# Sigmoid attention and a squared-ReLU MLP on one core: keys in tiles of 128 and a rest of 64, the rests of two pairs in quarters of the array

## The chip, the cores and the metric

The kernel runs on one core of a Trainium2 chip. Its time is the device time of one launch in microseconds. The engines are TensorE (PE; its weight loads are PEld), VectorE (DVE), ScalarE (ACT), GpSimd (POOL) and SyncE (SP), which issues all the DMAs of this kernel in one queue, in order.

## The reference

```python
# q, k, v: 8 batches, 12 heads, 448 positions, 64 wide; w_in 768 x 2048, w_out 2048 x 768
scores = np.matmul(q, k.transpose(0, 1, 3, 2)) / np.sqrt(64) - np.log(448)
attn = 1.0 / (1.0 + np.exp(-scores))
x = np.matmul(attn, v).transpose(0, 2, 1, 3).reshape(8 * 448, 768)
r = np.maximum(x @ w_in, 0.0)
out = (r * r) @ w_out
```

The attention weights are sigmoids, so no row is normalised. The two MLP weights arrive as 64-bit floats (two 32-bit words each) and are turned into 32-bit floats on the chip.

## The kernel before

**Attention.** The 12 heads of a batch are handled as 6 pairs, 48 pairs in all; two heads of 64 fill 128 partitions. `load_pair` brings q and k of a pair, transposed, as one tile of 128x896 (448 KB); `split_pair` makes a high and a low part of it in fp32r on VectorE. `scores` multiplies keys by queries: the 448 keys of a pair are cut into four tiles of 112 (`KT, NT = 112, 4`), and for each tile there are three products (high by high, low by high, high by low), each of them for the two heads j, in two halves of the array's rows. So a pair has 4 x 3 x 2 = 24 matmuls of 448 columns in `sc`, a PSUM tile of two banks in 3 buffers. ScalarE takes each tile through the sigmoid into `at`, and `attn_v` sums the four tiles of `at` against v into one PSUM bank `pav` (2 buffers) with 4 x 2 plain fp32 matmuls, the heads in two halves of the array's columns. `put_x` copies `pav` to SBUF on VectorE and stores it to `xd` in DRAM.

`step(n)` sets the order of all that: it loads x of pair n+4 and v of pair n+3, copies and stores the output of pair n-1, splits x of pair n+2, and issues the scores of pair n+1 and `attn_v` of pair n. So TensorE always has one pair's scores ahead of the previous pair's `attn_v`, and within one engine everything stands in the order of the code (`manual_schedule`).

**MLP weights.** Spread over steps 0 to 44, `weights(k)` converts one chunk of words at a time (`load_chunk`, tiles f): two ScalarE instructions (`convert_words`, L125 and L126), then in a later step three on VectorE and one on GpSimd (`convert_join`). Every third k, `sums` makes four sums of the blocks a11, a12, a21, a22 of 128x384 on VectorE and stores the seven blocks that the products need. 49 values of k lie on 45 steps, so that steps 0, 11, 22 and 33 have two of them.

**MLP.** Each of the two products is done for two batches at a time (a group g, four groups) with seven block products in place of eight (1 to 7 in the code), all in fp32r with three matmuls for one product. `gemm1` loads the weights of a block row from `w1`, `gemm2` from `w2`; `load_weights` brings 768 KB or 576 KB and `halve_weights` splits them into a high part (ScalarE, L170) and a low part (VectorE, L171). `x_operands(g)` loads the group's x from `xd` and makes the operands of the seven products by pieces (`make`: a cast and a subtraction for each of the blocks; `sub`: differences t1 to t4). For the first group the pieces stand in and behind the last attention steps, and between the first products (`FIRST_STEPS`, `between`); for the later groups they are made during the second product of the group before.

Tiles come from pools of equal buffers: `op2` (35 of 128x896), `op1` (20 of 128x448), `w` (8 of 128x1536).

Of the kernel before, what the change touches and what calls it, by code (L numbers as in the profile page):

```python
# [22 lines left out]
KT, NT = 112, 4  # L23
# [40 lines left out]
):  # L64

# [73 lines left out]
    def sums(m, i, a, s):  # L139

        if m == 0:
            a11, a12, a21, a22 = (a[:, n] for n in range(4))
        else:
            a11, a21, a12, a22 = (a[:, n] for n in range(4))
        s2, s3, s1, s4 = (s[:, n] for n in range(4))
        nc.vector.tensor_add(out=s1, in0=a21, in1=a22)
        nc.vector.tensor_sub(out=s2, in0=s1, in1=a11)
        nc.vector.tensor_sub(out=s3, in0=a11, in1=a21)
        nc.vector.tensor_sub(out=s4, in0=a12, in1=s2)
        if m == 0:  # L150
            nc.sync.dma_start(out=w1[i][:, 0:2], in_=a[:, 0:2])
            nc.sync.dma_start(out=w1[i][:, 2:6], in_=s)
            nc.sync.dma_start(out=w1[i][:, 6], in_=a[:, 3])
        else:
            d = w2.rearrange("n p i c -> p n i c")[:, :, i]
            nc.sync.dma_start(out=d[:, 0:2], in_=a[:, 0::2][:, 0:2])
            nc.sync.dma_start(out=d[:, 2:6], in_=s)
            nc.sync.dma_start(out=d[:, 6], in_=a[:, 3])

    def load_weights(src, name):  # L160
        n = src.shape[1]
        hi, lo = wide(name + "h", F32R)[:, :n], wide(name + "l", F32R)[:, :n]
        nc.sync.dma_start(out=lo.bitcast(F32), in_=src)
        return hi, lo

# [16 lines left out]
    def load_v(b, p):  # L184
        vt = op2(f"v_{b}_{p}").rearrange("p a s -> p (a s)")[:, : NT * P].rearrange("p (t d) -> p t d", d=P)
        nc.sync.dma_start(out=vt[:KT], in_=v[b, p])  # L186
        return vt
# [7 lines left out]
    def scores(ps, b, p, x):  # L195
        out = []
        for t in range(NT):
            sc = ps.tile([P, 2, 512], F32, tag="sc", bufs=3, name=f"sc_{b}_{p}_{t}")[:, :, :S]
            ks = slice(t * KT, (t + 1) * KT)
            for n, (kp, qp) in enumerate(((0, 0), (1, 0), (0, 1))):  # L200
                for j in range(2):
                    rows = slice(j * D, (j + 1) * D)
                    nc.tensor.matmul(  # L203
                        sc[:KT, j], x[kp][rows, 1, ks], x[qp][rows, 0], start=(n == 0), stop=(n == 2)
                    )
            at = op2(f"at_{b}_{p}_{t}")
            nc.scalar.activation(at[:KT], sc[:KT], AF.Sigmoid, bias=NEG_LOG_S, scale=SCALE)  # L207
            out.append(at)
        return out

    def attn_v(ps, b, p, at, vt):
        pav = ps.tile([P, 512], F32, tag="pav", bufs=2, name=f"pav_{b}_{p}")[:, :S]
        for t in range(NT):
            for j in range(2):
                nc.tensor.matmul(  # L215
                    pav[j * D : (j + 1) * D],
                    vt[:KT, t, j * D : (j + 1) * D],
                    at[t][:KT, j],
                    start=(t == 0),
                    stop=(t == NT - 1),  # L220
                )
        return pav

    def put_x(b, p, pav):
        x = op1(f"xo_{b}_{p}")
        nc.vector.tensor_copy(out=x, in_=pav)  # L226
        return lambda: nc.sync.dma_start(out=xd[b, p], in_=x)

    def split(raw, name, new, vector=False):
        hi, lo = new(name + "h", F32R), new(name + "l", F32R)  # L230
# [4 lines left out]
        nc.vector.tensor_sub(out=lo, in0=raw, in1=hi.bitcast(F32))  # L235
        return hi, lo

    def x_operands(g):
# [5 lines left out]
        def load(n, b, k):  # L244
            r2, r1 = op2(f"x{n}_{g}"), op1(f"y{n}_{g}")
# [3 lines left out]
            raw[n] = (r2, r1)  # L249
# [7 lines left out]
        def make(product, n, vector=False):  # L257
            (h2, l2), (h1, l1) = (split(r, f"{t}{n}_{g}", new, vector) for r, t, new in zip(raw[n], "xy", (op2, op1)))
            ops[product] = [(h2[:, 0], l2[:, 0]), (h2[:, 1], l2[:, 1]), (h1, l1)]

# [25 lines left out]
    x, vt, xs, at, pav, f64, w = {}, {}, {}, {}, {}, {}, {}  # L286
    stores = []
    ops = {}

    def weights(k):  # L290
# [11 lines left out]
        halves = halves[:, :DM], halves[:, DM:]  # L302
# [9 lines left out]
    def step(ps, n):  # L312
# [3 lines left out]
        if n + VA <= last:  # L316
            vt[n + VA] = load_v(*pairs[n + VA])
        if n > 0:
            store = put_x(*pairs[n - 1], pav.pop(n - 1))
            if n <= last - 3:  # L320
                store()
            else:
                stores.append(store)
        if n + SA <= last:
            xs[n + SA] = split_pair(*pairs[n + SA], x[n + SA])
        if n < last:
            at[n + 1] = scores(ps, *pairs[n + 1], xs[n + 1])
# [264 lines left out]
```

## Time and profile before

| | before |
|---|---|
| median of 3 runs (lowest to highest) | 1117.72 us (1116.38 to 1126.99) |
| the profiled execution | 1117.46 us |
| its span | 1115.4 us |
| granted TensorE clock | 1.0 |
| TensorE busy | 1105.8 us, 99% |
| VectorE, ScalarE, GpSimd busy | 70%, 55%, 5% |
| DMA | 202.32 MB, mean 181 GB/s over the span |

In lines of the profile, L12 is line 12 of the kernel; `out<-in` are the program's names with the buffer numbers left out; xN counts the instructions; behind a bar or in square brackets stands the idle time of the engine before them and what ended it. In the timeline the first number is the start and the second the length, in microseconds. In a row of stretches there stand, behind its limits and length, the busy time and instructions of PE, PEld, DVE, ACT and POOL, the granted clock, the DMA engines' share and GB/s. Matmuls overlap in the pipeline, so that the distance of their starts tells more than the length of one.

### The profile page before, as it was taken

The page shows a single profiled execution, that of the slowest core. Times are in us where ns is not written, and L with a number is a line of the kernel's source. Part 1 is how long each engine was busy: PE and PEld are TensorE (multiplying, and loading weights), DVE is VectorE, ACT ScalarE, POOL GpSimd, SP SyncE. Part 2 cuts the span into 40 slices and gives each one's busy share as a digit, 9 for nine tenths or more (in the row PEclk, how much of TensorE's full clock was granted, in tenths as well). Part 3 has the DMA queues.
Part 4 walks back from the last instruction along what each step waited for, and adds up shares of the span by engine and source line. Part 5 has one row for each costly group of instructions (what it writes and reads, how often), then busy time and mean ns, then how long its engine had stood idle before and what let it go on. Part 6 is the DMA issues. An engine that isn't in the chain of part 4 may idle for free.

```text
span 1115.4 us, 15057 instructions
## 1 busy us (share of the span) xinstructions
PE 1105.8 (99%) x5965; PEld 902.7 (81%) x5965; DVE 780.4 (70%) x873; ACT 611.9 (55%) x733; POOL 59.7 (5%) x36
## 2 busy tenths in 40 slices
PE   8999999999999999999999999999999999999998
PEld 4554544555699999999999999999999999999998
DVE  6778787877975499764558987355699845549951
ACT  6777777776653466543336565244546543346631
POOL 1212221221000000000000000000000000000000
PEclk9999999999999999999999999999999999999999
DMA  9989999999533344552332455333333653334431
GB/s 301 333 319 348 330 322 346 339 344 324 188 116 99 103 138 138 203 169 92 115 118 101 138 187 196 120 116 100 124 114 120 217 169 100 99 104 138 138 129 59
DMA packets 66503, 202.32 MB, mean 181 GB/s; under 512 B 6784, under 2 KB 33408, under 8 KB 66432
## 3 DMA queue, kind: packets, MB, share of 16 engines
q1 hardware_dynamic: 66432, 201.35, 52.9%
q8 instruction: 47, 0.77, 0.3%
q14 instruction: 24, 0.20, 0.1%
HBM read 157.29 MB, written 44.04 MB: 181 GB/s over the span
## 4 chain that ended last, share of the span: by engine, by line
PE 97%; DMA 1%; ACT 1%; DVE 0%; SPq 0%; issue 0%; ACTq 0%
PE ha L340 21%; PE oa L340 21%; PE pav L215 13%; PE sc L203 11%; PE ob L340 10%; PE hb L340 10%; PE hc L340 5%; PE oc L340 5%; DMA f<-w_in 1%; ACT at L207 0%; ACT a L125 0%; SPq L186 0%; ACT f L126 0%; SPq L181 0%; DVE xo L226 0%
## 5 line engine op out<-in xcount | busy, mean ns | idle before, releaser
L207 ACT ACTIVATE at<-sc 112x896 f32<-112x896 f32 x192 | 160.4, 923 | 71.5 <-PE sc L203 71.5
L171 DVE TENSOR_TENSOR w_1l<-w_1l,w_1h 128x1536 fp32r<-128x1536 f32 x58 | 101.8, 1755 | 81.8 <-ACT w_1h L170 81.7
L215 PE MATMUL pav<-at,v 112*64 112x448 f32 x768 | 154.7, 545 | 0.0
L367 ACT COPY s<-ha 128x448 f32<-128x448 f32 x96 | 51.1, 532 | 158.8 <-PE ha L340 136.6
L215 PEld LDWEIGHTS pav<-at,v 112*64 112x64 f32 x768 | 50.9, 136 | 82.5 <-issue 81.8
L170 ACT CAST w_1h<-w_1l 128x1536 fp32r<-128x1536 f32 x58 | 85.9, 1481 | 25.8 <-DMA w_1l<-w 25.7
L203 PE MATMUL sc<-qh 64*112 64x448 f32 x384 | 78.9, 407 | 3.6 <-ACT at L207 3.6
L203 PEld LDWEIGHTS sc<-qh 64*112 64x112 f32 x384 | 33.5, 170 | 51.7 <-issue 21.8
L170 ACT CAST w_0h<-w_0l 128x1536 fp32r<-128x1536 f32 x28 | 41.5, 1481 | 54.6 <-DMA w_0l<-w 54.6
L203 PE MATMUL sc<-qh,ql 64*112 64x448 f32 x384 | 70.6, 364 | 0.6 <-DVE ql L192 0.6
L137 POOL TENSOR_TENSOR a<-a,f 128x768 int32<-128x768 int32 x32 | 59.5, 1859 | 213.2 <-DVE a L134 128.7
L203 PE MATMUL sc<-ql,qh 64*112 64x448 f32 x384 | 70.3, 361 | 0.0
L400 DVE TENSOR_TENSOR g<-hb,s 128x448 f32<-128x448 f32 x32 | 19.9, 623 | 71.5 <-PE hb L340 71.5
L171 DVE TENSOR_TENSOR w_0l<-w_0l,w_0h 128x1536 fp32r<-128x1536 f32 x28 | 49.1, 1755 | 27.4 <-ACT w_0h L170 27.4
L226 DVE COPY xo<-pav 128x448 f32<-128x448 f32 x48 | 29.9, 623 | 54.5 <-PE pav L215 54.5
L170 ACT CAST w_5h<-w_5l 128x1152 fp32r<-128x1152 f32 x31 | 36.0, 1160 | 46.6 <-DMA w_5l<-w 42.6
L171 DVE TENSOR_TENSOR w_5l<-w_5l,w_5h 128x1152 fp32r<-128x1152 f32 x31 | 41.9, 1353 | 21.0 <-ACT w_5h L170 21.0
L192 DVE TENSOR_TENSOR ql<-x,qh 128x896 fp32r<-128x896 f32 x48 | 52.4, 1092 | 1.6
L363 DVE SCALAR_TENSOR_TENSOR g<-g 128x896 f32<-128x896 f32 x48 | 52.2, 1088 | 1.0
L191 DVE CAST qh<-x 128x896 fp32r<-128x896 f32 x48 | 40.1, 835 | 6.8 <-DMA x<-qk 6.8
L454 DVE TENSOR_TENSOR o<-ob,t 128x448 f32<-128x448 f32 x24 | 14.9, 620 | 33.2 <-PE ob L340 26.6
L203 PEld LDWEIGHTS sc<-ql,qh 64*112 64x112 f32 x384 | 33.6, 171 | 5.4
(649 smaller groups left out, 2958.6 us busy)
## 6 DMA issues: line engine op xcount, KB each, us to landing
w_1l<-w SPq DMA_DIRECT2D x58, 768.0 KB, 4.3
x<-qk SPq DMA_DIRECT2D x48, 448.0 KB, 7.3
w_0l<-w SPq DMA_DIRECT2D x28, 768.0 KB, 4.6
w_5l<-w SPq DMA_DIRECT2D x31, 576.0 KB, 4.2
f<-w_in SPq DMA_DIRECT2D x16, 768.0 KB, 6.5
w<-s SPq DMA_DIRECT2D x16, 768.0 KB, 4.0
f<-w_out SPq DMA_DIRECT2D x16, 768.0 KB, 6.4
v<-v SPq DMA_DIRECT2D x48, 224.0 KB, 7.2
```

The source lines that it names most:

```text
L137: nc.gpsimd.tensor_tensor(out=wb, in0=wb, in1=t.bitcast(I32)[:, :, 0], op=ALU.add)
L170: nc.scalar.copy(out=hi, in_=raw)
L171: nc.vector.tensor_sub(out=lo, in0=raw, in1=hi.bitcast(F32))
L191: nc.vector.tensor_copy(out=hi, in_=x)
L192: nc.vector.tensor_sub(out=lo, in0=x, in1=hi.bitcast(F32))
L203: nc.tensor.matmul(sc[:KT, j], x[kp][rows, 1, ks], x[qp][rows, 0], start=(n == 0), stop=(n == 2))
L207: nc.scalar.activation(at[:KT], sc[:KT], AF.Sigmoid, bias=NEG_LOG_S, scale=SCALE)
L215: nc.tensor.matmul(pav[j * D : (j + 1) * D], vt[:KT, t, j * D : (j + 1) * D], at[t][:KT, j], start=(t == 0), stop=(t == NT - 1),)
L226: nc.vector.tensor_copy(out=x, in_=pav)
L340: nc.tensor.matmul(out, a[:, c], b, start=first and n == 0, stop=last and n == 2, skip_group_check=True)
L363: nc.vector.scalar_tensor_tensor(out=t, in0=t, scalar=0.0, in1=t, op0=ALU.max, op1=ALU.mult)
L367: nc.scalar.copy(out=s, in_=banks["a", i])
```

## The change

It has three parts.

*The keys.* A pair's 448 keys are cut into three tiles of 128 and a rest of 64. The scores of the rest go through the sigmoid into one half of the partitions of a tile `rest`, which the two pairs of an even and an odd step share (the even one in partitions 0 to 63, the odd one in 64 to 127). `attn_v` sums the three full tiles; behind the odd pair's, `attn_v_rest` adds the rests of both pairs: four matmuls with 64 rows and 64 columns of the array each. v comes for two pairs in one load (seven tiles of 128x128). Both `pav` of a two-pair are copied and stored in the next even step.

*x kept on chip.* The outputs of the first two batches stay in 12 `op1` buffers and are not stored; the first group's operands are made from them, in pieces that are put into steps 28 to 46 by a table.

*Weight stores.* The seven blocks of a weight are stored as two DMAs (three blocks, four blocks) in place of three, and `w2` is laid out with the seven blocks of a row beside each other, as `w1` was. The second product's loads then read 4 pieces of 1536 B in a row of the partition, in place of one of 6144 B; the late blocks of `w1` come with two DMAs in place of one.

```diff
-KT, NT = 112, 4
+NT, KR = S // P, S % P
-XA, VA, SA, NWP = 4, 3, 2, 45
+XA, SA, NWP = 4, 2, 45
+KEPT = 2
+PIECES = {28: (1,), 32: (2,), 36: ("t1",), 40: (3,), 44: ("t2",), 45: (6,), 46: ("t3",)}
...
     def sums(m, i, a, s):
-        if m == 0:
-            nc.sync.dma_start(out=w1[i][:, 0:2], in_=a[:, 0:2])
-            nc.sync.dma_start(out=w1[i][:, 2:6], in_=s)
-            nc.sync.dma_start(out=w1[i][:, 6], in_=a[:, 3])
-        else:
-            d = w2.rearrange("n p i c -> p n i c")[:, :, i]
-            nc.sync.dma_start(out=d[:, 0:2], in_=a[:, 0::2][:, 0:2])
-            nc.sync.dma_start(out=d[:, 2:6], in_=s)
-            nc.sync.dma_start(out=d[:, 6], in_=a[:, 3])
+        to = (w1, w2)[m][i]
+        nc.sync.dma_start(out=to[:, 0:3], in_=a[:, 1:4] if m == 0 else a[:, 0:3])
+        nc.sync.dma_start(out=to[:, 3:7], in_=s)
...
     def scores(ps, b, p, x, rest):
-            ks = slice(t * KT, (t + 1) * KT)
+            keys = P if t < NT else KR
+            ks = slice(t * P, t * P + keys)
...
-            at = op2(f"at_{b}_{p}_{t}")
-            nc.scalar.activation(at[:KT], sc[:KT], AF.Sigmoid, bias=NEG_LOG_S, scale=SCALE)
-            out.append(at)
+            if t < NT:
+                at = op2(f"at_{b}_{p}_{t}")
+                out.append(at)
+            else:
+                at = rest[p % 2 * KR : (p % 2 + 1) * KR]
+            nc.scalar.activation(at, sc[:keys], AF.Sigmoid, bias=NEG_LOG_S, scale=SCALE)
...
+    def attn_v_rest(pavs, rest, vt):
+        for r in range(2):
+            for j in range(2):
+                rows, columns = slice(r * KR, (r + 1) * KR), slice(j * D, (j + 1) * D)
+                nc.tensor.matmul(
+                    pavs[r][columns], vt[rows, 2 * NT, columns], rest[rows, j], start=False, stop=True
+                )
...
+        if b < KEPT:
+            kept[b, p] = x
+            return lambda: None
...
     def step(ps, n):
         if n + XA <= last:
             x[n + XA] = load_pair(*pairs[n + XA])
-        if n + VA <= last:
-            vt[n + VA] = load_v(*pairs[n + VA])
-        if n > 0:
-            store = put_x(*pairs[n - 1], pav.pop(n - 1))
-            if n <= last - 3:
-                store()
-            else:
-                stores.append(store)
+            if n % 2 == 0:
+                b, p = pairs[n + XA]
+                vt[n // 2 + XA // 2] = load_v(b, p // 2)
+        if n % 2 == 0 and n > 0:
+            for m in (n - 2, n - 1):
+                store = put_x(*pairs[m], pav.pop(m))
+                if n <= last - 3:
+                    store()
+                else:
+                    stores.append(store)
...
-        pav[n] = attn_v(ps, *pairs[n], at[n], vt[n])
+        pav[n] = attn_v(ps, *pairs[n], at[n], vt[n // 2])
+        if n % 2:
+            attn_v_rest((pav[n - 1], pav[n]), rest[n // 2], vt[n // 2])
         for k in range(NK):
             if k * NWP // NK == n:
                 weights(k)
+        pieces_of(*PIECES.get(n, ()))
```

On TensorE in the middle of the attention, one pair's `attn_v` (pair 5 of batch 2) between two pairs' scores stood like this:

```order
L203 MATMUL sc_3_0_3_1282<-qh_3_0_1184 112x448 x2
L203 MATMUL sc_3_0_3_1282<-qh_3_0_1184,ql_3_0_1185 112x448 x2
L203 MATMUL sc_3_0_3_1282<-ql_3_0_1185,qh_3_0_1184 112x448 x2
L215 MATMUL pav_2_5_1291<-at_2_5_0_1195,v_2_5_1053 64x448 x2
L215 MATMUL pav_2_5_1291<-at_2_5_1_1204,v_2_5_1053 64x448 x2
L215 MATMUL pav_2_5_1291<-at_2_5_2_1213,v_2_5_1053 64x448 x2
L215 MATMUL pav_2_5_1291<-at_2_5_3_1222,v_2_5_1053 64x448 x2
L203 MATMUL sc_3_1_0_1319<-qh_3_1_1251 112x448 x2
```

The same engine in an odd step of the change (pairs 0 and 1 of batch 2):

```order
L215 MATMUL sc_2_2_3_979<-qh_2_2_893 64x448 x2
L215 MATMUL sc_2_2_3_979<-qh_2_2_893,ql_2_2_894 64x448 x2
L215 MATMUL sc_2_2_3_979<-ql_2_2_894,qh_2_2_893 64x448 x2
L231 MATMUL pav_2_1_987<-at_2_1_0_904,v_2_0_631 64x448 x2
L231 MATMUL pav_2_1_987<-at_2_1_1_913,v_2_0_631 64x448 x2
L231 MATMUL pav_2_1_987<-at_2_1_2_922,v_2_0_631 64x448 x2
L240 MATMUL pav_2_0_932<-rest_6_820,v_2_0_631 64x448 x2
L240 MATMUL pav_2_1_987<-rest_6_820,v_2_0_631 64x448 x2
```

The fourth `attn_v` tile of each pair has become a share of the four matmuls at L240; an even step has only the three rows of L231.

On VectorE, where the copies of `pav` (xo) stood one to a step, ahead of the splits of x (qh, ql) and the weight work (a, s):

```order
L226 COPY xo_2_2_1119<-pav_2_2_1098 128x448
L191 CAST qh_2_5_1122<-x_2_5_984 128x896
L192 TENSOR_TENSOR ql_2_5_1123<-x_2_5_984,qh_2_5_1122 128x896
L130 TENSOR_SCALAR a_5_1047<-a_5_1047 128x768
L131 TENSOR_SCALAR a_5_1047<-a_5_1047 128x768
L134 SCALAR_TENSOR_TENSOR a_5_1047<-f64_0_5_1_982,a_5_1047 128x768
L226 COPY xo_2_3_1181<-pav_2_3_1162 128x448
```

In the change two of them stand together and the next step has none:

```order
L249 COPY xo_2_2_1135<-pav_2_2_1057 128x448
L249 COPY xo_2_3_1138<-pav_2_3_1114 128x448
L200 CAST qh_3_0_1141<-x_3_0_1008 128x896
L201 TENSOR_TENSOR ql_3_0_1142<-x_3_0_1008,qh_3_0_1141 128x896
L155 TENSOR_TENSOR s_5_1005<-a_5_1004 128x384
L156 TENSOR_TENSOR s_5_1005<-s_5_1005,a_5_1004 128x384
L157 TENSOR_TENSOR s_5_1005<-a_5_1004 128x384
L158 TENSOR_TENSOR s_5_1005<-a_5_1004,s_5_1005 128x384
L200 CAST qh_3_1_1199<-x_3_1_1072 128x896
```

The copy of an even pair has moved one step later, behind the end of the odd one. At the start of SyncE's queue, the loads up to the second chunk of words (f64_0_0_1) were

```order
L181 DMA x_0_0_79<-qk 128x896
L186 DMA v_0_0_81<-v 112x512
L181 DMA x_0_1_83<-qk 128x896
L113 DMA f64_0_0_0_85<-w_in 128x1536
L181 DMA x_0_2_87<-qk 128x896
L186 DMA v_0_1_89<-v 112x512
L181 DMA x_0_3_91<-qk 128x896
L186 DMA v_0_2_93<-v 112x512
L113 DMA f64_0_0_1_95<-w_in 128x1536
```

and are now

```order
L190 DMA x_0_0_79<-qk 128x896
L190 DMA x_0_1_81<-qk 128x896
L195 DMA v_0_0_83<-v 128x896
L122 DMA f64_0_0_0_85<-w_in 128x1536
L190 DMA x_0_2_87<-qk 128x896
L190 DMA x_0_3_89<-qk 128x896
L122 DMA f64_0_0_1_91<-w_in 128x1536
L195 DMA v_0_1_93<-v 128x896
```

The second load of v has moved behind the second chunk of words.

More of the change, by code (lines that the diff above doesn't have):

```diff
@@ L193, in split_pair, with scores @@
         return hi, lo
-    def scores(ps, b, p, x):
+    def scores(ps, b, p, x, rest):
         out = []
-        for t in range(NT):
+        for t in range(NT + 1):
             sc = ps.tile([P, 2, 512], F32, tag="sc", bufs=3, name=f"sc_{b}_{p}_{t}")[:, :, :S]
-            ks = slice(t * KT, (t + 1) * KT)
+            keys = P if t < NT else KR
+            ks = slice(t * P, t * P + keys)
             for n, (kp, qp) in enumerate(((0, 0), (1, 0), (0, 1))):
@@ L214, in attn_v, with put_x, split_to @@
             for j in range(2):
+                columns = slice(j * D, (j + 1) * D)
                 nc.tensor.matmul(
[L216 to L220, printed above, removed]
-                )
-        return pav
-    def put_x(b, p, pav):
-        x = op1(f"xo_{b}_{p}")
-        nc.vector.tensor_copy(out=x, in_=pav)
+                    pav[columns], vt[:, p % 2 * NT + t, columns], at[t][:, j], start=(t == 0), stop=False
+                )
+        return pav
+    def attn_v_rest(pavs, rest, vt):
[5 more added lines that the diff above has]
+                )
+    def put_x(b, p, pav, scalar=False):
+        x = op1(f"xo_{b}_{p}")
+        if scalar:
+            nc.scalar.copy(out=x, in_=pav)
+        else:
+            nc.vector.tensor_copy(out=x, in_=pav)
+        if b < KEPT:
+            kept[b, p] = x
+            return lambda: None
         return lambda: nc.sync.dma_start(out=xd[b, p], in_=x)
-    def split(raw, name, new, vector=False):
-        hi, lo = new(name + "h", F32R), new(name + "l", F32R)
+    def split_to(hi, lo, raw, vector=False):
         if vector:
@@ L235, in split @@
         nc.vector.tensor_sub(out=lo, in0=raw, in1=hi.bitcast(F32))
+    def split(raw, name, new):
+        hi, lo = new(name + "h", F32R), new(name + "l", F32R)
+        split_to(hi, lo, raw)
         return hi, lo
@@ L244, in load @@
         def load(n, b, k):
+            if g == 0:
+                raw[n] = [kept[b, 3 * k + c] for c in range(3)]
+                return
             r2, r1 = op2(f"x{n}_{g}"), op1(f"y{n}_{g}")
@@ L257, in make @@
         def make(product, n, vector=False):
-            (h2, l2), (h1, l1) = (split(r, f"{t}{n}_{g}", new, vector) for r, t, new in zip(raw[n], "xy", (op2, op1)))
+            h2, l2 = (op2(f"x{n}_{g}{c}", F32R) for c in "hl")
+            if g == 0 and product in (1, 2, 3, 6):
+                both = op2(f"y{n}_{g}", F32R)
+                h1, l1 = both[:, 0], both[:, 1]
+            else:
+                h1, l1 = (op1(f"y{n}_{g}{c}", F32R) for c in "hl")
             ops[product] = [(h2[:, 0], l2[:, 0]), (h2[:, 1], l2[:, 1]), (h1, l1)]
+            parts = ops[product] if g == 0 else [(h2, l2), (h1, l1)]
+            for x, (hi, lo) in zip(raw[n], parts):
+                split_to(hi, lo, x, vector)
         load("11", 0, 0)
@@ L285, in sigmoid_attention_relu2_mlp @@
     todo = [(m, i) for m in range(2) for i in range(NI)]
-    x, vt, xs, at, pav, f64, w = {}, {}, {}, {}, {}, {}, {}
+    x, vt, xs, at, pav, f64, w, rest = {}, {}, {}, {}, {}, {}, {}, {}
     stores = []
+    pieces = {}
     ops = {}
@@ L331, in step, with next_scores, pieces_of @@
                 weights(k)
+        pieces_of(*PIECES.get(n, ()))
+    def next_scores(ps, n):
+        if n % 2 == 0:
+            rest[n // 2] = op2(f"rest_{n // 2}")
+        at[n] = scores(ps, *pairs[n], xs[n], rest[n // 2])
+    def pieces_of(*names):
+        for name in names:
+            pieces[name]()
     def bank(name):
@@ L376, in run @@
             out = banks[k, i]
-            hi, lo = weights[i, PLACE[n] >= PH]
-            at = PLACE[n] % PH
+            late, at = SPOT[n]
+            hi, lo = weights[i, late]
             w = tuple(t[:, at].rearrange("p (c m) -> p c m", m=P) for t in (hi, lo))
@@ L443, in operands @@
             ops[n] = out
+            blocks_of = w2.rearrange("i p n c -> n p i c")[PLACE[1][n]]
             weights[n] = [
[L445 removed]
+                halve_weights(load_weights([blocks_of[:, h * PH : (h + 1) * PH]], f"w2_{g}_{n}_{h}"))
+                for h in range(2)
             ]
@@ L496, in ahead @@
                 for piece in pieces.values():
-                    piece(False)
+                    piece()
         return ahead
```

117 lines of the change are left out of this document (61 added, 56 removed).

## The prediction

> **What bounds the kernel now.** I read the page's first part, the chain, and then stretches of the program.
>
> ```profile
> span 1115.4 us, 15057 instructions
> PE 1105.8 (99%) x5965; PEld 902.7 (81%) x5965; DVE 780.4 (70%) x873; ACT 611.9 (55%) x733; POOL 59.7 (5%) x36
> PE ha L340 21%; PE oa L340 21%; PE pav L215 13%; PE sc L203 11%; PE ob L340 10%; PE hb L340 10%; PE hc L340 5%; PE oc L340 5%; DMA f<-w_in 1%; ACT at L207 0%; ACT a L125 0%; SPq L186 0%; ACT f L126 0%; SPq L181 0%; DVE xo L226 0%
> L215 PE MATMUL pav<-at,v 112*64 112x448 f32 x768 | 154.7, 545 | 0.0
> L226 DVE COPY xo<-pav x48: 615/625/626, 16.3 to 293.3; 128x448 f32<-128x448 f32 x48
> 320.00:380.00 60.00, 60.00 (x297) 55.59 (x297) 33.74 (x35) 23.80 (x32) 0.00 (x0) 1.00 0.34 110
> ```
>
> TensorE is the chain nearly everywhere. From 294 us on it is full (60.00 of 60.00 us), and the change leaves those products' matmuls as they are, so the gain must come from the attention steps, 16.3 to 293.3 us by the copies of `pav`: 277.0 / 47 = 5.89 us a step. One step, in the timeline of TensorE and its weight loads:
>
> ```profile
> 100.57 0.46 PE L203 MATMUL sc<-qh 64*112 64x448 f32 x2
> 100.86 0.37 PE L203 MATMUL sc<-qh,ql 64*112 64x448 f32 x2
> 101.07 0.36 PE L203 MATMUL sc<-ql,qh 64*112 64x448 f32 x2
> 102.28 0.37 PE L203 MATMUL sc<-ql,qh 64*112 64x448 f32 x2
> 102.51 0.46 PE L203 MATMUL sc<-qh 64*112 64x448 f32 x2
> 102.81 0.36 PE L203 MATMUL sc<-qh,ql 64*112 64x448 f32 x2
> 103.01 0.36 PE L203 MATMUL sc<-ql,qh 64*112 64x448 f32 x2
> 103.30 3.23 PE L215 MATMUL pav<-at,v 112*64 112x448 f32 x16
> 106.45 0.46 PE L203 MATMUL sc<-qh 64*112 64x448 f32 x2
> ...
> 12.26 0.14 PEld L215 LDWEIGHTS pav<-at,v 112*64 112x64 f32 x2 [0.23 <-issue]
> 12.64 0.14 PEld L215 LDWEIGHTS pav<-at,v 112*64 112x64 f32 x2 [0.23 <-issue]
> 13.01 0.14 PEld L215 LDWEIGHTS pav<-at,v 112*64 112x64 f32 x2 [0.23 <-issue]
> ```
>
> Scores go two at a time (x2), a pair every 0.20 us; 12 pairs. Each of the 8 `attn_v` matmuls is two instructions (768 for 48 x 8). Their weight loads go in twos, one for each half of the columns, every 0.375 us: 8 slots, 3.0 us. Where the array changes from one use to the other, slots are longer: from 103.01 to 103.30 is 0.29, not 0.20, and the `attn_v` stretch, 103.30 to 106.45, is 3.15, not 3.0; behind it the first score pair takes 0.29. I put 0.14 us on the way from scores to `attn_v` (0.09 of gap and 0.05 on the first slot, 3.15 less 3.0 being both ends together) and 0.19 on the way back (0.09 of gap, 0.10 on the first pair). The fourth score tile waits for a bank that ScalarE frees: 102.28 to 102.51 to 102.81 is 0.53 for two slots, 0.12 too many. 2.43 + 3.0 + 0.14 + 0.19 + 0.12 = 5.88, the step.
>
> **The rests in quarters.** (Step n issues the scores of pair n+1 and `attn_v` of pair n; even and odd go by n.) Two pairs had 16 slots of `attn_v`. Now each has 6 (three key tiles), and the four matmuls of the rests, 8 instructions, follow the odd one. If all four quarters work at once these are 2 slots. 16 - 14 = 2 slots of 0.375, 0.75 us for two steps; 24 times, 18.0 us. No row shows a quarter. Bounds: 2 slots if all are independent, 4 if only two run at a time, as the halves do. I take 2, the independent case, since rows show both halvings work: scores in two halves of the rows, `attn_v` in two halves of the columns, and 16 instructions in 3.23 us is 8 slots and a tail, so no half waits for the other's second pass.
>
> The score tiles become 128 and 64 keys wide. A pair still streams 448 columns, as the tiles of 112 did, and the count (24 for a pair) stays: nothing there. What the narrower fourth tile may cost is another change of the array's use, at a place that has 0.12 us of waiting now. Priced like scores to `attn_v`, 0.14, it adds 0.02 to 0.03: 48 x 0.03 = 1.4 us; bounds: -0.05 a tile (a shorter weight load) to +0.10 (the gap comes on top). Going from `attn_v` to the rests is a change too, 24 times: nothing to 0.20, I take 0.14: 3.4 us. A row that has this price is 103.30 above. The Trainium skill, TensorEngine Tiling, Key Properties, says that a change of tiling mode drains the engine; the 0.14 and 0.19 agree with that, and by it both new changes cost, while without it the gain would be 4.8 us larger.
>
> **ScalarE.**
>
> ```profile
> 101.53 3.34 ACT L207 ACTIVATE at<-sc 112x896 f32<-112x896 f32 x4 [0.91 <-PE sc L203]
> ...
> 82.23 0.95 ACT L125 ACTIVATE a<-f 128x768 f32<-128x768 f32 x1
> 83.03 0.95 ACT L126 ACTIVATE f<-f 128x768 int32<-128x768 uint32 x1
> 84.83 0.46 PE L203 MATMUL sc<-qh 64*112 64x448 f32 x2 [0.40 <-ACT at L207]
> ...
> PE sc L203 <- ACT at L207: 3.6, 4, 2.4
> ...
> L234 ACT CAST y_1h<-y 128x448 fp32r<-128x448 f32 x3 | 1.7, 562 | 0.1
> ```
>
> A step's sigmoids take 3.34 us (896 elements in a row before and after, whatever the partitions), a pair of word conversions 82.23 to 83.98, 1.75: 5.1 us. The even step falls to about 5.2 (5.89 + 0.03 - 2 x 0.375 = 5.17), the odd one is 5.17 + 0.75 + 0.14 = 6.06. So ScalarE still fits, with nothing to spare in even steps. Three steps (11, 22, 33) hold two word conversions: 6.84 us of ScalarE, and each costs 0.4 us now (3.6 in four waits, 2.4 of them at the start). Steps 11 and 33 are odd, a little longer than now, about 0.3 each; 22 is even, 0.7 us shorter, so about 1.1. Step 28 is even and gets the first of the moved x pieces behind a conversion: three casts of 128x448 at 0.562, 3.34 + 1.75 + 1.69 = 6.78, so 1.1 again. The pieces of steps 32 and 40 meet no conversion (3.34 + 1.69 = 5.03): free. Together 2.8 us for 1.2 now: +1.6, bounds 0 to 4.
>
> **VectorE and the two `pav` banks.** Both of a two-pair's `pav` now end together, behind the rests, and are copied one behind the other at the start of the even step. TensorE's next `attn_v` needs the first copy; ahead of it lie the next pair's scores.
>
> ```profile
> DVE xo L226 <- PE pav L215: 54.5, 36, 1.6
> ...
> L191 DVE CAST qh<-x 128x896 fp32r<-128x896 f32 x48 | 40.1, 835 | 6.8 <-DMA x<-qk 6.8
> 200.00:250.00 50.00, 49.58 (x338) 25.18 (x336) 39.52 (x56) 37.74 (x47) 13.03 (x7) 1.00 0.96 343
> ```
>
> VectorE has 39.52 of 50 us, 4.66 a step, 9.3 of the new 11.2 for two; it idles up to 1.6 us ahead of the copy now. With the copy ready 0.75 us into the even step (0.12 after the last matmul, and 0.625) and wanted at 2.73 (100.57 to 103.30), it may be 2.0 us late before TensorE waits. Behind a late copy stand the casts of x two steps ahead and the weight sums, which have as long. A moved piece adds three subtractions of 128x448, 1.9 us, in seven steps; the pair's 1.9 spare takes it. I price this at nothing; if that cover is gone, see the rivals.
>
> **DMA.** The queues carry 0.96 of their time, 343 GB/s, so a step that is 5% shorter needs a lighter load: 12 of 48 stores of x (224 KB each) and the first group's reads of them (12 x 224 KB again) go, and `v` comes in 24 loads of 448 KB for 48 of 224 KB, no fewer bytes. A step of pair 12 on carries 1.97 MB as before (x 0.46, v 0.23, xd 0.23; 32 chunks of words and 16 lots of seven weight blocks over 45 steps, 0.56 and 0.49), in 5.62 us 350 GB/s against 334 in 5.89. What pays for that are the rows of the stores: 1536 B become 4608 and 6144. I cost it at nothing, as loads are issued four pairs ahead. The second product's weights now come in rows of 1536 B:
>
> ```profile
> w_1l<-w SPq DMA_DIRECT2D x58, 768.0 KB, 4.3
> 593.29 0.32 SPq L163 DMA_DIRECT2D w_1l<-w  x1
> 598.42 1.48 ACT L170 CAST w_1h<-w_1l 128x1536 fp32r<-128x1536 f32 x1
> 600.57 1.75 DVE L171 TENSOR_TENSOR w_1l<-w_1l,w_1h 128x1536 fp32r<-128x1536 f32 x1
> 603.31 0.36 PE L340 MATMUL oa<-o_2h,w_1h 128*128 128x448 f32 x1
> ```
>
> The tightest one is split by 602.32 and used at 603.31: 1.0 us of slack in the split alone, and its load (593.29 and 4.3 us, so 597.6) lies 0.8 ahead of the cast. It would have to get about 40% slower to be felt, four times for a microsecond or so. Nothing.
>
> **Start and seam.**
>
> ```profile
> 16.96 0.90 ACT L125 ACTIVATE a<-f 128x768 f32<-128x768 f32 x1 [1.93 <-DMA f<-w_in]
> 19.50 0.46 PE L203 MATMUL sc<-qh 64*112 64x448 f32 x2 [2.42 <-ACT at L207]
> 0.00:15.00 15.00, 13.21 (x79) 6.56 (x79) 6.12 (x9) 9.46 (x11) 0.20 (x4) 1.00 0.88 269
> 293.99 0.47 PE L340 MATMUL ha<-x_0h,w_firsth 128*128 128x448 f32 x1 [0.72 <-DVE xo L226]
> ```
>
> The first steps wait for the second chunk of words. Ahead of it now go 3008 KB, not 3232 (one load of two pairs' v, not three of one): 224 KB at 269 GB/s, 0.8 us earlier. The first two-pair's 0.75 drowns in this wait. The seam to the products costs 0.72 us for the last copy and keeps it (one copy on each engine). The pieces that left the seam were hidden there.
>
> **Sum:** -23 x 0.75 (17.3) - 0.8 + 1.4 + 3.4 + 1.6 = -11.7 us. The profiled execution took 1117.46 us, 0.26 less than the median shown; 1117.46 - 11.7 = **1105.8 us**. Taking every bound's end, this case reaches from 1117.5 - 18.1 - 2.4 = 1097 to 1117.5 - 18.1 + 4.8 + 4.8 + 4 = 1113.
>
> **Rivals.**
> - *Strict order between quarters.* If an instruction may not start ahead of an earlier one that waits, the passes overlap in a chain, and the rests are 3 slots: 24 x 0.375 = 9.0 back, 1114.8 us. The 3.23 us for 16 instructions speak against it (a chain would be 9 slots, 3.6). 10%. The Trainium skill, TensorE: Matmul & The Clock Gate, Part 3, says matmuls start and end strictly in order; that rule gives this rival, and the 3.23 us do not bear it out for columns.
> - *Only two quarters at a time*, the other side: rests 4 slots, all 18 us gone, and the changes of use stay: 1117.5 + 6.4 - 0.8 = 1123 us, 1130 with the upper ends of the changes (4.8 and 4.8) and of ScalarE (4). It turns to a loss at 4 slots, since 3 still pay. For it: no row has quarters. 7%.
> - *The copy of both banks comes late.* If VectorE is over 2.0 us late in even steps, TensorE waits; 1 us each, 23 times, gives 1129 at most, half of the steps 1117. For it: 9.3 of 11.2 us in order, now with two copies in one burst. Against: 1.6 us idle ahead of copies. 6%.
> - *Transfers set the step.* If 343 GB/s is all there is, 1.97 MB need 5.74 us, for the 32 steps after the kept ones 0.12 more each: 4 us, 1110. 9%; the step's casts of x would wait for DMA.
>
> **Chances.** Forecast 68%, rivals as above. About 1% is what a measurement of this kernel tells from no change: 1106.5 us is the line. Of the forecast's own range somewhat over two thirds lies below it, 0.48; with a little of the rest, faster by over 1%: 0.50. Slower by over 1% needs 1129, the last ends of two rivals: 0.05. Within: 0.45. The range 1098 to 1116 holds the forecast, the strict order and slow transfers, and leaves out the other two and the extremes.
>
> **What would show it.** `attn_v` stretches of 6 slots, 2.4 us; a rests stretch of 8 instructions in about 0.9 us (2 slots and a tail of 0.17), 1.3 with three, 1.65 with four; two steps in 11.2 us; gaps at the fourth tile of about 0.14; TensorE's waits for ScalarE about 1 us at steps 22 and 28; none for `xo`; casts of x not waiting for DMA; the products' part, from the seam to the end, 821 us (1115.4 - 294.0) as now. I would be wrong if a rests stretch takes over 1.2 us, or if a step waits for something that it does not wait for now.

## The result, and the profile after

| | before | after |
|---|---|---|
| median (lowest to highest), six runs each on one chip | 1120.33 us (1116.38 to 1126.99) | 1109.21 us (1104.21 to 1112.2) |
| ratio, 95% interval | | 0.989 [0.985, 0.993] |
| again on another chip | 1117.6 us | 1106.71 us (1105.86 to 1111.09), 0.990 [0.989, 0.992] |
| the profiled execution, its span | 1117.46, 1115.4 us | 1108.67, 1106.9 us |
| first matmul of the products (the seam) | 293.99 us | 280.84 us |
| from there to the end of the span | 821.4 us | 826.1 us |

The change is 11 us faster, and the forecast of 1105.8 lies 3.4 us below the first median. That is nearer than its terms deserve: to the seam the program gained 13.2 us where the sum had 11.7, and the products, which were to stay as they were, lost 4.7 us. The 0.3 us that remain lie outside the span.

The page of the change, first lines:

```profile
span 1106.9 us, 15055 instructions
PE 1094.7 (99%) x5965; PEld 893.6 (81%) x5965; DVE 798.2 (72%) x879; ACT 617.0 (56%) x745; POOL 63.4 (6%) x36
```

The number of matmuls is the same, 5965, and TensorE is busy 11.1 us less: what it lost is slots (the 0.375 us from one pair of `attn_v` instructions to the next), not instructions. Two steps in the timeline of TensorE, with its first number the start; an odd step from 104.89, an even one from 110.92:

```profile
102.49 2.48 PE L231 MATMUL pav<-at,v 128*64 128x448 f32 x12
104.89 0.47 PE L215 MATMUL sc<-qh 64*128 64x448 f32 x2
...
106.62 0.37 PE L215 MATMUL sc<-ql,qh 64*128 64x448 f32 x2
106.84 0.42 PE L215 MATMUL sc<-qh 64*64 64x448 f32 x2
...
107.60 2.48 PE L231 MATMUL pav<-at,v 128*64 128x448 f32 x12
110.01 0.98 PE L240 MATMUL pav<-rest,v 64*64 64x448 f32 x8
110.92 0.47 PE L215 MATMUL sc<-qh 64*128 64x448 f32 x2
...
112.64 0.37 PE L215 MATMUL sc<-ql,qh 64*128 64x448 f32 x2
112.85 0.37 PE L215 MATMUL sc<-qh 64*64 64x448 f32 x2
...
113.55 2.48 PE L231 MATMUL pav<-at,v 128*64 128x448 f32 x12
```

Read starts, not lengths. The rests take 110.01 to 110.92, 0.91 us for 8 instructions. The odd step is 104.89 to 110.92, 6.03; the `attn_v` stretches of two even steps start at 102.49 and 113.55, so two steps take 11.06 us, where they took 11.76 before (two of 5.88). From the start of one `attn_v` stretch to that of the next, the steps take 5.11 and 5.97 us at the median, and 5.89 before.

What TensorE waits for, from the view of waits (engine, tile and line, what ended the wait; us in total, times, the longest):

```profile
PE sc L215 <- ACT at L223: 4.7, 5, 1.5
...
PE pav L231 <- DVE xo L249: 1.1, 2, 0.6
PE ha L395 <- DVE xo L249: 0.8, 1, 0.8
PE ha L395 <- DVE w_5l L181: 0.3, 1, 0.3
PE sc L215 <- DVE ql L201: 0.3, 1, 0.3
```

Before, these were 3.6 us in four waits for ScalarE, 0.6 for `ql` and 0.7 for the last `xo`. ScalarE's share has grown by 1.1 us although the one at the start became 0.95 shorter (2.42, now 1.47), and VectorE's waits for `xo` in the middle of the attention are new.

### The profile page after: what moved, and what is told of

Its sections match the earlier page's. It is cut to its first block, busy times and chain, and to the rows that moved or that the text cites. A ratio compares the mean times of both kernels' runs of the same rounds, so it can differ in the third digit from the quotient of the medians.

```text
span 1106.9 us, 15055 instructions
## 1 busy us (share of the span) xinstructions
PE 1094.7 (99%) x5965; PEld 893.6 (81%) x5965; DVE 798.2 (72%) x879; ACT 617.0 (56%) x745; POOL 63.4 (6%) x36
## 4 chain that ended last, share of the span: by engine, by line
PE 91%; ACT 4%; DVE 3%; issue 1%; DMA 0%; ACTq 0%; DVEq 0%
PE oa L395 21%; PE ha L395 21%; PE ob L395 11%; PE hb L395 10%; PE sc L215 8%; PE pav L231 8%; PE hc L395 5%; PE oc L395 5%; PE pav L240 2%; ACT at L223 1%; DVE ql L201 1%; ACT rest L223 1%; ACT f L135 1%; DVE qh L200 0%; PE warm_ps L562 0%
## 5 line engine op out<-in xcount | busy, mean ns | idle before, releaser
L223 ACT ACTIVATE at<-sc 128x896 f32<-128x896 f32 x144 | 121.6, 921 | 51.6 <-PE sc L215 51.4
L231 PE MATMUL pav<-at,v 128*64 128x448 f32 x576 | 118.6, 547 | 1.1 <-DVE xo L249 1.1
L180 ACT CAST w_1h<-w_1l 128x1536 fp32r<-128x1536 f32 x58 | 85.9, 1480 | 23.8 <-DMA w_1l<-w 23.7
L231 PEld LDWEIGHTS pav<-at,v 128*64 128x64 f32 x576 | 37.2, 136 | 63.2 <-issue 58.7
L215 PE MATMUL sc<-qh 64*128 64x448 f32 (+1 forms) x384 | 77.2, 399 | 4.7 <-ACT at L223 4.7
L146 POOL TENSOR_TENSOR a<-a,f 128x768 int32<-128x768 int32 x32 | 63.2, 1976 | 198.6 <-DVE a L143 135.8
L215 PEld LDWEIGHTS sc<-qh 64*128 64x128 f32 (+1 forms) x384 | 33.3, 170 | 50.9 <-ACT at L223 16.3
L201 DVE TENSOR_TENSOR ql<-x,qh 128x896 fp32r<-128x896 f32 x48 | 71.1, 1480 | 1.6
L215 PE MATMUL sc<-qh,ql 64*128 64x448 f32 (+1 forms) x384 | 70.2, 362 | 0.3 <-DVE ql L201 0.3
L215 PE MATMUL sc<-ql,qh 64*128 64x448 f32 (+1 forms) x384 | 70.3, 362 | 0.0
L223 ACT ACTIVATE rest<-sc 64x896 f32<-64x896 f32 x48 | 43.7, 909 | 0.6
```

Of the source, the lines that this page charges most:

```text
L146: nc.gpsimd.tensor_tensor(out=wb, in0=wb, in1=t.bitcast(I32)[:, :, 0], op=ALU.add)
L180: nc.scalar.copy(out=hi, in_=raw)
L201: nc.vector.tensor_sub(out=lo, in0=x, in1=hi.bitcast(F32))
L215: nc.tensor.matmul(sc[:keys, j], x[kp][rows, 1, ks], x[qp][rows, 0], start=(n == 0), stop=(n == 2))
L223: nc.scalar.activation(at, sc[:keys], AF.Sigmoid, bias=NEG_LOG_S, scale=SCALE)
L231: nc.tensor.matmul(pav[columns], vt[:, p % 2 * NT + t, columns], at[t][:, j], start=(t == 0), stop=False)
```

## The experiments

Each has four to seven runs and is compared with runs of the kernel before on the same chip. `keys_only`, `all_but_keys`, `same_rows` and `spread` ran on one chip (median of the kernel before 1117.75 us), the other four on another (1117.6).

**Which part earns it.** `keys_only` is the kernel before with the first part alone (tiles of 128 and 64, quarters, v of two pairs in one load): x goes to DRAM as before, and the weight stores and pieces are the old ones. Against the change:

```diff
-KEPT = 2
...
-PIECES = {28: (1,), 32: (2,), 36: ("t1",), 40: (3,), 44: ("t2",), 45: (6,), 46: ("t3",)}
...
-        to = (w1, w2)[m][i]
-        nc.sync.dma_start(out=to[:, 0:3], in_=a[:, 1:4] if m == 0 else a[:, 0:3])
-        nc.sync.dma_start(out=to[:, 3:7], in_=s)
...                                  # the three stores of w1 and of w2 as before
-        if b < KEPT:
-            kept[b, p] = x
-            return lambda: None
```

> The keys in tiles of 128 and 64 with the rests in quarters, and nothing else of the change: x of all batches goes through DRAM, the operand pieces and the weight stores stay as before. Theory (the rests in quarters are the gain, the transfers keep up without the other parts): two steps take 11.1 us, the attention part is 11 to 14 us shorter than before, time ratio to before 0.988 to 0.990. Rival (transfers would set the step without the lighter load: 1.97 MB a step at 343 GB/s is 5.74 us): two steps 11.5 us, casts of x wait for DMA, ratio 0.994 to 0.997.

`all_but_keys` is the reverse: tiles of 112 and one `attn_v` of 8 matmuls, with x kept and the new stores.

```diff
-NT, KR = S // P, S % P
+KT, NT = 112, 4
...
-        if n % 2:
-            attn_v_rest((pav[n - 1], pav[n]), rest[n // 2], vt[n // 2])
```

> The other half: four tiles of 112 keys as before, but x of two batches kept on chip, the operand pieces in the steps, and weight stores in longer rows. Theory: steps of 5.89 us as before, the seam keeps its 0.7 us, and the step that has a piece behind a word conversion costs about a microsecond; ratio 0.999 to 1.002. Rival (the kept x shortens the seam or frees transfers that TensorE waits for): 3 to 5 us less, ratio 0.996.

`keys_only` took 1101.41 us (1100.04 to 1103.13), a ratio of 0.985 [0.984, 0.987]; `all_but_keys` 1121.01, 1.003 [1.002, 1.005]. The first part alone gains 16.3 us (0.988 to 0.990 was expected), and the two others together gain nothing by themselves: they are 3.3 us slower (0.999 to 1.002 was expected). On another chip the change and `keys_only` ran again, unchanged, as `after_again` and `keys_again`.

> The changed kernel itself once more, beside the keys alone on one chip. Theory (the keys alone carry the gain, and the pieces of x in the steps give 3.9 us of it back, as the seam at 280.84 against 276.95 us says): 3 to 6 us slower than the keys alone, ratio to before 0.988 to 0.991. Rival (the two were measured on different chips and are equal): within 1 us of the keys alone, ratio 0.985 to 0.986. A profile of it also shows whether a stretch of TensorE with matmuls 206.7 ns apart in place of 202.7 comes back at another time.

> The keys alone once more, for the comparison with the three others on this chip: seam at 277 us, ratio to before 0.984 to 0.987 by either theory.

They took 1106.71 us (0.990 [0.989, 0.992]) and 1103.6 us (0.987 [0.985, 0.989]): 3.1 us apart, and the fastest run of the one (1105.86) is slower than the slowest of the other (1104.51). In the waits of `keys_only` the rows of VectorE inside the attention are gone:

```profile
PE sc L206 <- ACT at L214: 3.4, 4, 1.4
...
PE ha L363 <- DVE xo L240: 0.8, 1, 0.8
```

and its seam is at 276.95 us, 17.0 earlier than before and 3.9 earlier than in the change. `all_but_keys` has its seam at 293.18, 0.8 earlier than before; what it loses lies behind the seam (829.4 us of products). 1.0 us of that are waits (0.7 for `w_5l`, 0.3 for ScalarE); in two stretches its matmuls are slower as described at the end, which no run ties to this edit. So how much of its loss is the edit's stays open; that the extras cost rests on the change against `keys_only`.

**Whether the quarters work together.** `same_rows` puts the odd pair's rest into the even pair's rows, so that only two quarters can be used at a time. It then multiplies by the even pair's rest of v, so the odd pairs' output lacks its own; the instructions and their sizes are those of the change. The two rests then need a tile each.

```diff
-                at = rest[p % 2 * KR : (p % 2 + 1) * KR]
+                at = rest[p % 2][:KR]
...
-                rows, columns = slice(r * KR, (r + 1) * KR), slice(j * D, (j + 1) * D)
+                rows, columns = slice(0, KR), slice(j * D, (j + 1) * D)
...
-                    pavs[r][columns], vt[rows, 2 * NT, columns], rest[rows, j], start=False, stop=True
+                    pavs[r][columns], vt[rows, 2 * NT, columns], rest[r][rows, j], start=False, stop=True
...
-            rest[n // 2] = op2(f"rest_{n // 2}")
+            rest[n // 2] = op2(f"rest_{n // 2}"), op2(f"rest2_{n // 2}")
```

> As the change, but the rests of both pairs lie in the same half of the array's rows (the odd pair's rest is multiplied with the even pair's rows of v, so its output is left wrong there), so that only two of the four matmuls can run side by side. Theory (four quarters run at once in the change): the rests' stretch grows from 0.91 us to about 1.65, two steps from 11.1 to 11.8, and the time by 24 x 0.75 = 18 us, to about 1122 to 1127, no better than before. Rival (the gain comes from the three wide key tiles and not from running four quarters): the stretch stays at 0.9 us and the time within 3 us of the change.

1120.86 us, 1.003 [1.002, 1.005], a little less than the 1122 to 1127 expected, with the seam at 294.40. Its timeline in an odd step:

```profile
99.78 0.36 PE L215 MATMUL sc<-ql,qh 64*128 64x448 f32 x2
99.98 0.38 PE L215 MATMUL sc<-qh 64*64 64x448 f32 x2
100.19 0.37 PE L215 MATMUL sc<-qh,ql 64*64 64x448 f32 x2
...
100.70 2.48 PE L231 MATMUL pav<-at,v 128*64 128x448 f32 x12
103.10 1.72 PE L240 MATMUL pav<-rest,v 64*64 64x448 f32 x8
104.75 0.47 PE L215 MATMUL sc<-qh 64*128 64x448 f32 x2
```

The same 8 instructions take 1.65 us instead of 0.91, the 4 slots of the second rival; 0.74 in each of 24 odd steps is 17.8 us, of which 13.6 show at the seam. The longer steps cover other waits: those for ScalarE are 3.2 us for 4.7, and VectorE's 1.4 in the attention are gone, 2.9 of the 4.2 between. So without the four quarters working at once nothing of the gain is left: the seam is 0.4 us later than before. The single records also show the order of starts. The program has the even pair's four instructions first, and the last of them signals that its bank is done. In `same_rows` this one is the fourth of the eight to start, in the change the sixth, in all 24 odd steps: two instructions of the odd pair start ahead of it. The Trainium skill, TensorE: Matmul & The Clock Gate, Part 3, has matmuls start and end strictly in order; for the starts of plain fp32 matmuls in quarters the rule does not hold here (ends are modelled in the trace and say nothing).

**Whether ScalarE's doubled steps can be mended by moving them.** In the change, the worst waits follow from steps 22 (137 us) and 28 (172 us). Rows of ScalarE and TensorE in the timeline there, in order of time:

```profile
137.48 0.92 ACT L134 ACTIVATE a<-f 128x768 f32<-128x768 f32 x1
...
139.10 0.90 ACT L134 ACTIVATE a<-f 128x768 f32<-128x768 f32 x1
139.91 0.90 ACT L135 ACTIVATE f<-f 128x768 int32<-128x768 uint32 x1
140.70 2.52 ACT L223 ACTIVATE at<-sc 128x896 f32<-128x896 f32 x3
141.65 0.41 PE L215 MATMUL sc<-qh 64*64 64x448 f32 x2 [1.46 <-ACT at L223]
...
173.81 1.02 ACT L259 CAST x_0h<-xo 128x448 fp32r<-128x448 f32 x2
174.73 0.56 ACT L259 CAST y<-xo 128x448 fp32r<-128x448 f32 x1
175.20 2.52 ACT L223 ACTIVATE at<-sc 128x896 f32<-128x896 f32 x3
176.16 0.42 PE L215 MATMUL sc<-qh 64*64 64x448 f32 x2 [1.24 <-ACT at L223]
```

Two conversions (137.48 to 140.81), or one and a piece's casts, stand ahead of the next sigmoids; the fourth score tile waits until the first of these has freed its bank. `spread` has the doubled places one step later (1, 12, 23, 34), where they hold one conversion and not two (of every three numbers k the third converts nothing on ScalarE), some pieces in other steps, and the first halving of a weight one step later.

```diff
+SHIFT = 4
...
-PIECES = {28: (1,), 32: (2,), 36: ("t1",), 40: (3,), 44: ("t2",), 45: (6,), 46: ("t3",)}
+PIECES = {29: (1,), 32: (2,), 37: ("t1",), 40: (3,), 43: ("t2",), 45: (6,), 46: ("t3",)}
...
-            if k * NWP // NK == n:
+            if (k * NWP + SHIFT) // NK == n:
...
+            step(ps, last - 1)
             halve_weights(first[0, False])
-            step(ps, last - 1)
```

> As the change, with ScalarE's bunched work spread: the steps with two conversion stages hold the second and third stage, of which only one is a ScalarE conversion, the first operand piece moves from step 28 to 29, which has no conversion, the t pieces to odd steps, and the first halving of weights one step later. Theory (TensorE's 4.7 us of waits for sigmoids come from these bunches, and 1.4 us of waits for pav and ql from VectorE's): the three long waits of 1.2 to 1.5 us go, 3 to 4 us less than the change, ratio to before about 0.986. Rival (the waits only move, since ScalarE and VectorE are nearly full in these steps): waits of the same sum in other steps, VectorE's for pav above all, and no change.

1104.58 us, 0.988 [0.987, 0.990]; seam at 279.40, only 1.4 us earlier than the change, where 3 to 4 were expected. Its waits:

```profile
PE pav L232 <- DVE xo L250: 3.7, 3, 2.2
PE sc L216 <- DVE ql L202: 2.2, 3, 1.1
```

No wait for ScalarE is left, and 5.9 us of waits for VectorE have come in its place. The longest, in the timeline:

```profile
223.38 3.36 DVE L286 TENSOR_TENSOR xo<-xo,xo 128x448 f32<-128x448 f32 x3
226.66 1.14 DVE L250 COPY xo<-pav 128x448 f32<-128x448 f32 x2
227.32 0.97 PE L232 MATMUL pav<-at,v 128*64 128x448 f32 x4 [2.16 <-DVE xo L250]
```

A piece's subtractions stand ahead of the copies that free the two `pav` banks. So most of the loss only moved, from one engine's full steps to the other's full queue.

**Whether the pieces in the steps cost it.** `late_pieces` is the change with its pieces behind the last steps and at the seam, x still on chip.

```diff
-PIECES = {28: (1,), 32: (2,), 36: ("t1",), 40: (3,), 44: ("t2",), 45: (6,), 46: ("t3",)}
+PIECES = {}
...
             step(ps, last - 2)
+            pieces[1](True)
...
             step(ps, last - 1)
+            pieces[2](True)
+            pieces_of("t1")
             step(ps, last)
+            pieces_of(3, "t2")
...
+            pieces_of(6)
...
+            lambda: pieces_of("t3"),
```

> As the change (kept x, two stores, wide rows), but the first group's operand pieces stand behind the last steps and between the first products, where they stood before, and not in steps 28 to 46. Theory (the pieces in the steps cost what the change loses against the keys alone, by ScalarE at step 28 and by VectorE from step 33 on): the steps 28 to 46 go back to 11.1 us for two, the seam comes at 277 to 278 us, 3 to 4 us less than the change; the 0.5 us wait for the late blocks of w1 stays. Rival (kept buffers or the other rows of the stores cost it): the seam stays near 280.5 us and the time that of the change.

1107.75 us, 0.991 [0.989, 0.993]: no better than the change on the same chip (1106.71). The steps from 28 on take about 5.1 and 5.97 us again (step 33, doubled, 6.41), but the seam, at 278.97 where 277 to 278 was expected, pays:

```profile
278.97 0.49 PE L395 MATMUL ha<-x_0h,w_firsth 128*128 128x448 f32 x1 [2.58 <-ACT yt L259]
```

2.58 us, for casts of a piece that is made at the last moment, in place of 0.80. From start to start of the `attn_v` stretches, the steps are 3.8 us shorter than in `after_again`; 1.8 of it is lost again at the seam, which lies 2.0 us earlier (280.97 there). The products then take 2.4 us longer (826.4 for 824.0), with equally long slow stretches of the kind described at the end. A wait of 0.65 us in them is one reason. The other is the clock just behind the pause (a row of windows: limits, length, busy us and matmuls of PE, granted clock, DMA share, GB/s):

```profile
279.20:282.60 3.40, 3.40 (x10) 0.50 0.37 135
```

Up to 282.62 us nine matmuls come 0.37 us apart in place of 0.20, 1.5 us in all; in the change the like stretch behind the seam (280.84 to 284.20) has 17 matmuls at a clock of 1.00. No other profile here has a lower clock between its start and its end, but that the pause brings it on was not tried apart. So the pieces in the steps do cost most of what the change lies behind `keys_only` at the seam (3.8 of about 4 us); this other place costs as much.

**A version without the waits.** `odd_doubles` is `keys_only` with the steps that hold two numbers k at 1, 15, 23 and 37 instead of 0, 11, 22 and 33.

```diff
+DOUBLE = (1, 15, 23, 37)
...
+    STEP_OF = [k - sum(k > d + i for i, d in enumerate(DOUBLE)) for k in range(NK)]
...
-            if k * NWP // NK == n:
+            if STEP_OF[k] == n:
```

> The keys alone, and the four steps that have two stages of the weights' conversion become odd steps (1, 15, 23, 37) that hold the second and third stage, of which one converts on ScalarE. Theory (the steps of 7.61, 5.53 and 5.51 us are waits for ScalarE's doubled conversions): the waits of 1.6, 0.5 and 0.5 us go, about 2.5 us less than the keys alone, ratio to before about 0.983. Rival (VectorE, which then waits for a conversion of the same step, is late with the copies of pav in the next even step): waits for xo of 0.5 to 1 us four times, and no change against the keys alone.

1098.26 us (1096.44 to 1100.34), 0.982 [0.980, 0.984], the fastest of all. Its waits, and a row of its windows (limits, length, busy us and instructions of PE, PEld, DVE, ACT, POOL, granted clock, DMA share, GB/s):

```profile
PE ha L365 <- DVE xo L241: 0.8, 1, 0.8
```

```profile
200.00:250.00 50.00, 50.00 (x360) 25.46 (x362) 46.12 (x61) 42.54 (x52) 13.70 (x7) 1.00 1.00 355
```

The first fence is its only wait behind the warm-up in the view of waits, for the last copy at the seam (272.80 us); up to there TensorE does not stop, not even at the start. Of three numbers k in a row only two have a conversion on ScalarE. Here, as in `spread`, those that share a step are the second and third, so that no step has two conversions, and the step is always an odd one, the longer. `keys_again` beside it took 1103.6 us, 5.3 more, where 2.5 were expected. The seam of `keys_only` is 4.15 us later. Its steps 0, 11, 22 and 33 are 1.5, 0.5, 1.6 and 0.5 us longer than the others of their kind, 4.0 in all; the view counts 3.4 of this as waits for ScalarE, because it counts from the end of a matmul (0.36 us after its start, where the next would have started 0.20 after). For ScalarE the missing second conversion is what counts: `spread` has the same numbers together in steps 1, 12, 23 and 34, two of them even, and no wait for ScalarE either. Whether the odd step matters, for VectorE say, was not tried apart.

## Why the prediction was right or wrong

The profiled executions differ by 8.8 us: 13.15 gained to the seam, 4.65 lost behind it, 0.3 outside the span. By the steps of the sum, up to the seam:

| step | forecast | measured |
|---|---|---|
| the steps themselves (quarters, fourth tile, change into the rests) | -17.3 + 1.4 + 3.4 = -12.5 | 23 x (11.06 - 11.76) = -16.1 |
| start | -0.8 | 1.47 - 2.42 = -0.95 |
| ScalarE, the other steps | +1.6 | 3.3 - 1.2 = +2.1 |
| VectorE | 0 | 1.1 + 0.3 + 0.8 - 0.6 - 0.7 = +0.9 |
| sum | -11.7 | -14.1, and -13.15 seen |

The rows of waits are as the view counts them, which is less than they cost, and the last odd step is in none of the rows. From start to start of the `attn_v` stretches nearly all has its place: 23 pairs of steps without a wait took 2 x 5.89 us and take 5.11 + 5.97 (-16.1); the steps with waits lost 4.2 us beyond that and lose 7.7 now (+3.5); from the last stretch to the seam it took 6.96 and takes 6.45 (-0.5). Together that is -13.1.

**Quarters: right.** The rests take 0.91 us where 0.9 was said, and `same_rows` shows that 4 slots take the whole gain away. Strict order and two at a time are both refuted. The rival of strict order was priced too low, though: by the chain that gives 9 slots for the 8 matmuls of `attn_v`, the 4 matmuls of the rests take 5, not 3, and 27 us would go back, not 9.

**Change into the rests: right in size.** An odd step's `attn_v` and rests take 107.60 to 110.92, 3.32, an even one's 102.49 to 104.89, 2.40; with 0.15 for the two old ends each, 3.32 - 0.15 - 8 x 0.375 leaves 0.17, for the 0.14 that was priced.

**The narrow fourth tile: the term that failed.** It was to cost another 0.03 us each, because a change of use came on top of a wait of 0.12. From the last pair ahead of it to `attn_v` is 1.02 us before (102.28 to 103.30), 0.98 in the odd step and 0.91 in the even step now (106.62 to 107.60, 112.64 to 113.55). That is 0.15 less in two steps, 3.5 us in 23, where the sum had 1.4 more: a little below the lower bound of -0.05 each. What went is the wait of 0.12, wholly in the even step and in part in the odd one. Rows of `same_rows` show that the change of use itself costs about nothing: where this tile does not wait there, the pairs start at 99.78, 99.98 and 100.19, the usual 0.20. The Trainium skill, TensorEngine Tiling, Key Properties, says that a change of tiling mode drains the engine; the ways into `attn_v` and into the rests do cost 0.14 to 0.17, and 64 rows by 128 columns to 64 by 64 costs nothing. Whether this last one is a change of mode for the array, no row tells.

**ScalarE: right in mechanism, somewhat small.** The forecast had 1.1 at steps 22 and 28; the waits are 1.46 and 1.24, and about 0.3 from steps 11 and 33 each, as said. In `spread` and `odd_doubles`, where no step has two conversions, the waits of steps 11, 22 and 33 are gone: the doubled work was the cause.

**VectorE "at nothing": wrong.** In the first part alone it held: `keys_only` has no such wait. In the change TensorE waits for `xo` in the middle of the attention, 1.1 us in two waits: a step waits for something that it did not wait for before, which the prediction had named as a sign of being wrong. With the pieces in the steps VectorE has 48.87 of 50 us (it had 39.52, and `keys_only`, the second row, has 45.59):

```profile
200.00:250.00 50.00, 48.94 (x350) 24.31 (x348) 48.87 (x66) 40.95 (x51) 11.88 (x6) 1.00 0.91 334
200.00:250.00 50.00, 49.73 (x364) 25.34 (x364) 45.59 (x62) 40.88 (x50) 11.91 (x6) 1.00 0.98 350
```

The spare 1.9 us of two steps, which was to take a piece, was about 1.0 already with the keys alone (45.59 of 50 is 10.1 in 11.08). The subtraction `ql` takes 1480 ns in the mean, for 1092 (1610 in `keys_only`), and the cast ahead of it 759 for 835:

```profile
L201 DVE TENSOR_TENSOR ql<-x,qh 128x896 fp32r<-128x896 f32 x48 | 71.1, 1480 | 1.6
```

and in the timeline the late copies of step 34 stand behind work that was held up (two subtractions of a piece in 2.84 us, where one takes 0.62 alone) and behind the doubled weight work of step 33:

```profile
196.42 2.84 DVE L260 TENSOR_TENSOR x_0l<-xo,x_0h 128x448 fp32r<-128x448 f32 x2
196.46 2.31 POOL L146 TENSOR_TENSOR a<-a,f 128x768 int32<-128x768 int32 x1 [4.91 <-ACT x_0h L259]
...
205.44 1.15 DVE L249 COPY xo<-pav 128x448 f32<-128x448 f32 x2
...
206.11 2.48 PE L231 MATMUL pav<-at,v 128*64 128x448 f32 x12 [0.46 <-DVE xo L249]
```

The prediction's rival of late copies had the place right and put it in all even steps; it decided in two.

**DMA: right.** Casts of x wait for DMA at the start alone (5.6 us, twice). `keys_only`, without the lighter load, has the same time for two steps, and `odd_doubles` keeps TensorE full with the queues at 1.00 of their time and 355 GB/s. Transfers do not set the step at this length. The stores' new rows are not tested alone.

**Products, 821 us: wrong by 4.65.** 0.5 us is the wait at 298.25 us for `w_5l` (0.35 by the view, and the 0.16 that each wait costs beyond it), whose load is now two DMAs; the prediction spoke of the other product's weights only. Some 4.1 us are slower matmuls, below, which no run ties to the change.

## What to carry to other kernels

Small fp32 matmuls that use a quarter of the array each are worth pairing up: 8 instructions took the time of 2 and a tail, but only when all four quarters get work. When TensorE's step shrinks, recount each other engine's work by the new step at the fullest steps, with durations as they are beside GpSimd: the keys alone were worth 16 us, and parts that were to lighten the DMA and the seam gave 3 to 5 of it back. Where two lots of work must share a step, pair those that load different engines: with that the seam came 4.15 us earlier than with the keys alone.

## What the runs showed of the hardware that was not expected

**Slower stretches at full granted clock.** The same row of windows over the products (limits, length, busy us and matmuls of PE, granted clock, DMA share, GB/s), in the change

```profile
380.00:480.00 100.00, 100.00 (x485) 1.00 0.49 161
480.00:590.00 110.00, 110.00 (x534) 1.00 0.33 112
```

and in `keys_again`, whose products take 821.6 us:

```profile
380.00:480.00 100.00, 100.00 (x495) 1.00 0.47 155
480.00:590.00 110.00, 110.00 (x544) 1.00 0.37 118
```

Full, without a wait, at a clock of 1.00, TensorE does 485 and 534 matmuls where it does 495 and 544: they come 206.7 ns apart, not 202.7. In the change this lasts from about 381 to 589 us and takes 20 matmuls' time, 4.1 us. It is not tied to a kernel: `keys_only` has it for about 100 us (products 823.45) and `keys_again`, the same kernel, nowhere; `after_again` has it from 898 to 996 us, not at 381. The chain of the change shows it in pieces of equal work:

```profile
473.25 14.88 PE ob L395 x72
...
679.84 14.59 PE ob L395 x72
```

What starts it stays open. It is a good part of a spread such as 1104.21 to 1112.2 for one kernel: differences of 2 to 4 us between single executions say nothing here, and the seams tell more than the totals.

**VectorE and GpSimd hold each other up.** A subtraction of 1.09 us takes 2.66 when GpSimd's add began shortly before it:

```profile
158.63 1.09 DVE L201 TENSOR_TENSOR ql<-x,qh 128x896 fp32r<-128x896 f32 x1
...
161.91 2.15 POOL L146 TENSOR_TENSOR a<-a,f 128x768 int32<-128x768 int32 x1 [4.68 <-DVE a L143]
...
162.35 2.66 DVE L201 TENSOR_TENSOR ql<-x,qh 128x896 fp32r<-128x896 f32 x1
```

The second ends at 165.01, 0.95 after GpSimd's end (164.06), so it seems to have waited for nearly all of it. In the change 12 of the 48 subtractions begin during an add, and each of them ends 0.95 us after that add; the other 36 take 1.09. The Trainium skill, SBUF — State Buffer, Who interferes with whom, says that a VectorE instruction with two inputs in SBUF and a GpSimd instruction that reads SBUF exclude each other, and that the later one blocks; these rows agree. Which of VectorE's instructions meets the 32 adds is a matter of the order: before, it was the cast alone (8 of 48 held up, no subtraction). In the other direction, the adds of the change that begin during a cast or a subtraction take 2.03 to 2.32 us, the others 1.84 to 1.89.
